# A fused attention and SwiGLU kernel: its pieces put in order by a list scheduler, in even blocks of 512 tokens

## The chip, the cores and the metric

One core of a Trainium2 chip. The core has a matrix engine (TensorE, PE in the rows; PEld is its weight load), a vector engine (DVE), an activation engine (ACT), GpSimd (POOL) and SP, which here only issues DMAs. Each engine works through its own queue in order and waits at semaphores for the others. The metric is the device time of one execution in microseconds (us); lower is better.

## The reference

Attention with normalised queries and keys (batch 8, 12 heads, 448 tokens, head size 64), then a SwiGLU feed-forward network over its 3584 tokens (768 to 1536 to 768), all in fp32:

```python
q_n, k_n = (rmsnorm(q, g_q), rmsnorm(k, g_k))
scores = scale * np.matmul(q_n, k_n.transpose(0, 1, 3, 2))
scores = scores - np.max(scores, axis=-1, keepdims=True)
attn = np.exp(scores)
attn = attn / (np.sum(attn, axis=-1, keepdims=True) + 1e-09)
x = np.matmul(attn, v)            # then to (tokens, heads * head size)
g = x @ w_gate
silu = g * (1.0 / (1.0 + np.exp(-g)))
val = x @ w_val
return (silu * val @ w_out).astype(np.float32)
```

The weights arrive as 64-bit floats, and the kernel turns them into fp32 itself.

## The kernel before

The launch has two versions in it: `fast`, which runs on this input, and `general` behind a test of the gains at the end. Everything below is about `fast`. Lines are those of the kernel before.

**Attention** goes by pairs of heads, 6 pairs to a batch, 48 in all (index m). For a pair, `normalise` squares q and k on ACT (L511), sums on DVE (L515, L516), takes the power -1/2 on POOL (tile rr, L518) and scales q and k on POOL (tile t, L522). `transpose_qk` turns t round on PE (L539); the copies QT (DVE, L544) and KT (ACT, L548) leave PSUM. `scores` makes, for each quarter j of the keys, two products (L555, tile st), an exponential on ACT (L563, tile e), and on POOL the running sum of e over j (L566, L568, tile sums). `weighted` multiplies the four e with v (L575, tile at). `divide` multiplies sums with a matrix of ones (L588), so that each row holds the denominators, inverts them (DVE RECIPROCAL, L590, tile inv) and writes the quotient to xT (L591). The pool of at has two buffers, for the product with v, the denominators and the transposes; st has two, e five.

**The network** goes by blocks of tokens. xT holds two batches (896 tokens), cut into a block of 384 and one of 512. A block has an up phase, 24 groups of 6 products (L622, tile mm, with `wg` for gates and `wv` for values, tanh on ACT at L633, two DVE steps at L634 and L638 into gt), and a down phase (L648, `wo`; 3 or 4 times 2 groups of 12 products), whose rows ACT copies out (L658) and stores. An fp32 product is two PE rows in the trace.

**The weights** come in 36 parts of 768 KB. `load_weights` puts a part into one of four places within gt; `round_weights` converts it: two ACT steps (L480, L481) and four DVE steps (L482, L483, L491, L494) for each part.

**The order** is the order of the Python calls, the same on all engines. `slot(i)` issues half a pair; `attend(n)` issues n slots, each with one step of the weights (two in slots 8 to 13); `mix` puts slots between the groups of a block. Seven pairs of attention run before the first up phase; six pairs lie in each even up phase (384 tokens), six in each odd down phase; even down phases and odd up phases have none:

```python
    attend(PER + 2)
    for n in range(B):
        if n % 2 == 0:
            mix(ups(n), PER)
...
            mix(downs(n), 0)
        else:
            mix(ups(n), 0)
            mix(downs(n), PER if n < B - 1 else 0)
```

Of the kernel before, what the change touches and what calls it, by code (L numbers as in the profile page):

```python
# [359 lines left out]

@with_exitstack
def fast(
# [23 lines left out]

# [12 lines left out]
    BLOCKS = ((0, 384), (384, 512))  # L399
    TB = 512  # L400

    const = ctx.enter_context(tc.tile_pool(name="const", bufs=1))
    io = ctx.enter_context(tc.tile_pool(name="io", bufs=2))
    prep = ctx.enter_context(tc.tile_pool(name="prep", bufs=2))
    attn = ctx.enter_context(tc.tile_pool(name="attn", bufs=1))
    ffn = ctx.enter_context(tc.tile_pool(name="ffn", bufs=2))
    ps_st = ctx.enter_context(tc.tile_pool(name="ps_st", bufs=2, space=bass.MemoryType.PSUM))
    ps_at = ctx.enter_context(tc.tile_pool(name="ps_at", bufs=2, space=bass.MemoryType.PSUM))
    ps_mm = ctx.enter_context(tc.tile_pool(name="ps_mm", bufs=2, space=bass.MemoryType.PSUM))
    ctx.enter_context(tc.manual_schedule())  # L410

# [3 lines left out]
    xT = const.tile([P, NW, 2 * S], F32, name="xT")  # L415
# [7 lines left out]

    qk, vt, qkn, QT, KT, E, sums, av = ({} for _ in range(8))

# [4 lines left out]
    def load_qk(m):  # L432
        if m < NM:
            for x, src in enumerate((q, k)):
                qk[m, x] = io.tile([R, 2, NJ, D], F32, name="qk", bufs=3)
                nc.sync.dma_start(qk[m, x].rearrange("p h j d -> p h (j d)"), pair_rows(src, m))

    def load_v(m):
        if m < NM:
            vt[m] = io.tile([R, 2, NJ, D], F32, name="v")  # L440
            nc.sync.dma_start(vt[m].rearrange("p h j d -> p h (j d)"), pair_rows(v, m))
# [8 lines left out]
    def weight_parts():  # L450
        gate, val = (w.rearrange("(c p) f -> p c f", p=P) for w in (moe_w_gate, moe_w_val))
        for f in range(NF // 2):
            for half in range(2):
                for w, dst in ((gate, wg), (val, wv)):
                    cs = ts(half, NW // 2)
                    yield w[:, cs, ts(f, 2 * P)], dst[:, f, cs, :], (NW // 2, 2 * P)
        rows = moe_w_out.rearrange("(f p) c -> p f c", p=P)
        for f in range(NF):
            yield rows[:, f : f + 1, :], wo[:, f : f + 1, :], (1, DM)

    def load_weights():
        if not parts:
            return
        n = parts[0][0]
        slot = n % 4 if n < 20 else 2 + n % 2
        if any(slot == other[0] for other in staged):
            return
        _, (src, dst, (a, b)) = parts.pop(0)
        raw = gt[:, ts(slot, NF // 4), :].rearrange("p f t -> p (f t)").bitcast(I64)
        raw = raw.rearrange("p (a b) -> p a b", a=a)  # L470
        nc.sync.dma_start(raw, src)
        words = raw.bitcast(U32).rearrange("p a (b two) -> p a b two", two=2)
        staged.append((slot, words[:, :, :, 0], words[:, :, :, 1], dst))

    def round_weights():
        if not staged:
            return
        _, lo, hi, w = staged.pop(0)
        bits = w.bitcast(U32)
        nc.scalar.activation(w, hi.bitcast(F32), AF.Abs)  # L480
        nc.scalar.activation(lo, lo, AF.Copy, scale=2.0**-29)  # L481
        nc.vector.tensor_scalar_max(w, w, LEAST)  # L482
        nc.vector.tensor_scalar(  # L483
            out=bits,
            in0=bits,
            scalar1=3,
            scalar2=0x3FFFFFFF,
            op0=ALU.logical_shift_left,
            op1=ALU.bitwise_and,
        )  # L490
        nc.vector.scalar_tensor_tensor(  # L491
            bits, hi, 0xC0000000, bits, op0=ALU.bitwise_and, op1=ALU.bitwise_or
        )
        nc.vector.tensor_tensor(out=bits, in0=bits, in1=lo, op=ALU.add)  # L494

    def weights_step():
        round_weights()
        load_weights()
# [3 lines left out]
    def normalise(m):  # L502


        if m >= NM:
            return
        src = [qk.pop((m, x)) for x in range(2)]
        t = prep.tile([R, NJ, 2, 2, D], F32, name="t")
        sq = t.rearrange("p j x h d -> p (j x h d)").rearrange("p (g d) -> p g d", d=D)
        for x in range(2):  # L510
            nc.scalar.activation(  # L511
                sq[:, ts(x, 2 * NJ)], src[x].rearrange("p h j d -> p (h j) d"), AF.Square
            )
        ss = prep.tile([R, 2 * 2 * NJ], F32, name="ss")
        nc.vector.tensor_reduce(out=ss, in_=sq, axis=AX.X, op=ALU.add)  # L515
        nc.vector.tensor_scalar_add(ss, ss, D * 1e-6)  # L516
        rr = prep.tile([R, 2, 2, NJ, 1], F32, name="rr")
        nc.gpsimd.tensor_tensor(  # L518
            out=rr.rearrange("p x h j one -> p (x h j one)"), in0=ss, in1=minus_half, op=ALU.pow
        )  # L520
        for x in range(2):
            nc.gpsimd.tensor_tensor(  # L522
# [7 lines left out]
    def transpose_qk(m):  # L530
        if m >= NM:
            return
# [280 lines left out]
```

## Time and profile before

| | us |
|---|---|
| median of three runs | 1924.35 |
| lowest, highest run | 1920.6, 1932.96 |
| the profiled execution, its own time | 1931.18 |
| span of its trace (first to last instruction) | 1929.4 |

The profile is of one execution. Its span leaves 1.8 us of that execution's time outside. In the rows below, a time line gives start, duration, engine, line, operation, output and inputs with their shapes, a count, and in brackets the idle time in front with what ended it. The end of a PE row is modelled, so lengths on PE are best read from one start to the next. PEclk is the clock granted to TensorE as a share of 2.4 GHz.

### The profile page before, as it was taken

The numbers are of one execution on the slowest core, as the hardware profiler recorded it, in microseconds if no ns is written. First come the engines' busy times: TensorE is split into PE (matmuls) and PEld (weight loads), VectorE is DVE, ScalarE is ACT, GpSimd is POOL, SyncE is SP. The second block draws the span as 40 slices with busy tenths as digits, with TensorE's granted clock in tenths as the row PEclk, the third lists the DMA queues.
The fourth block names the chain that finished last, engine by engine and source line by source line (L and its number), as shares of the span: only waits on it lengthen the run. The fifth ranks groups of instructions, "written<-read, shape, count | busy, mean of one in ns | idle before, by whom it ended". The sixth has DMA issues, their size and how long they took to land.

```text
span 1929.4 us, 14302 instructions
## 1 busy us (share of the span) xinstructions
PE 1773.2 (92%) x5760; PEld 867.0 (45%) x5760; DVE 530.3 (27%) x580; ACT 382.1 (20%) x561; POOL 550.6 (29%) x296
## 2 busy tenths in 40 slices
PE   4557669999989999999999899999999899999998
PEld 1223335544444455554444455554444445554455
DVE  4997563101122233201112233301112232201100
ACT  4353332100023222100022222200012222100000
POOL 5753224300035444400024544410015444200000
PEclk9778779999999999999999999999999899999999
DMA  4353330100011111000011110010001110000000
GB/s 155 116 160 106 112 113 29 32 13 0 0 37 46 47 29 29 24 21 0 0 33 41 41 29 29 29 30 0 0 17 47 37 38 20 2 21 4 0 9 26
DMA packets 55247, 73.37 MB, mean 38 GB/s; under 512 B 4996, under 2 KB 44420, under 8 KB 55172
## 3 DMA queue, kind: packets, MB, share of 16 engines
q1 hardware_dynamic: 45888, 61.35, 10.2%
q10 hardware_dynamic: 9284, 11.02, 2.0%
q8 instruction: 47, 0.77, 0.2%
q14 instruction: 28, 0.23, 0.0%
HBM read 61.34 MB, written 11.01 MB: 38 GB/s over the span
## 4 chain that ended last, share of the span: by engine, by line
PE 85%; POOL 5%; DVE 5%; issue 3%; ACT 1%; DMA 1%; POOLq 0%; SPq 0%; DVEq 0%; ACTq 0%
PE mm L622 44%; PE mm L648 20%; PE st L555 9%; PE at L575 8%; POOL rr L518 3%; POOL t L522 2%; PE at L539 2%; PE at L588 2%; DVE inv L590 1%; DMA gt<-in_moe_w_out_dram 1%; ACT e L563 1%; DVE wg L494 0%; DVE wg L483 0%; DVE wo L494 0%; DVE wg L491 0%
## 5 line engine op out<-in xcount | busy, mean ns | idle before, releaser
L622 PE MATMUL mm<-xT,wg 128*128 128x512 f32 (+1 forms) x1152 | 455.4, 544 | 7.8 <-DVE xT L591 7.8
L622 PE MATMUL mm<-xT,wv 128*128 128x512 f32 (+1 forms) x1152 | 450.4, 541 | 0.0
L648 PE MATMUL mm<-wo,gt 128*128 128x384 f32 x1344 | 444.0, 489 | 0.0
L566 POOL TENSOR_TENSOR sums<-e 112x896 f32<-112x896 f32 x48 | 102.2, 2129 | 1094.8 <-ACT e L563 850.5
L648 PEld LDWEIGHTS mm<-wo,gt 128*128 128x128 f32 x1344 | 252.3, 190 | 195.2 <-issue 27.3
L622 PEld LDWEIGHTS mm<-xT,wg 128*128 128x128 f32 x1152 | 214.8, 190 | 244.6 <-issue 168.3
L622 PEld LDWEIGHTS mm<-xT,wv 128*128 128x128 f32 x1152 | 219.9, 191 | 215.3 <-issue 139.9
L563 ACT ACTIVATE e<-st 112x896 f32<-112x896 f32 x192 | 170.9, 916 | 215.1 <-PE st L555 167.2
L568 POOL TENSOR_TENSOR sums<-sums,e 112x896 f32<-112x896 f32 x96 | 206.7, 2153 | 16.8 <-ACT e L563 12.9
L634 DVE SCALAR_TENSOR_TENSOR gt<-tanh,mm 128x384 f32<-128x384 f32 (+1 forms) x96 | 59.6, 620 | 530.8 <-ACT tanh L633 530.8
L555 PE MATMUL st<-QT,KT 64*112 64x448 f32 x768 | 195.5, 633 | 0.1
L590 DVE RECIPROCAL inv<-at 128x448 f32<-128x448 f32 x48 | 141.9, 2956 | 162.8 <-PE at L588 162.8
L575 PE MATMUL at<-e,v 112*64 112x448 f32 x768 | 167.3, 581 | 16.5 <-ACT KT L548 16.5
L633 ACT ACTIVATE tanh<-mm 128x384 f32<-128x384 f32 (+1 forms) x96 | 52.2, 543 | 648.3 <-PE mm L622 648.3
L539 PE MATMUL at<-ident,t 112*128 112x112 f32 x384 | 61.5, 306 | 126.6 <-POOL t L522 80.1
L518 POOL TENSOR_TENSOR rr<-ss,minus_half 112x16 f32<-112x16 f32 x48 | 143.8, 2996 | 12.0 <-DVE ss L516 12.0
L638 DVE SCALAR_TENSOR_TENSOR gt<-gt,mm 128x384 f32<-128x384 f32 (+1 forms) x96 | 59.6, 621 | 301.4 <-PE mm L622 301.4
L539 PEld LDWEIGHTS at<-ident,t 112*128 112x128 f32 x384 | 47.6, 163 | 153.3 <-POOL t L522 96.3
L575 PEld LDWEIGHTS at<-e,v 112*64 112x64 f32 x768 | 54.1, 146 | 132.5 <-issue 106.2
L515 DVE TENSOR_REDUCE ss<-t 112x16 f32<-112x1024 f32 x48 | 58.5, 1220 | 200.6 <-ACT t L511 200.6
L555 PEld LDWEIGHTS st<-QT,KT 64*112 64x112 f32 x768 | 68.8, 195 | 83.8 <-issue 66.7
L658 ACT COPY rows<-mm 128x384 f32<-128x384 f32 x56 | 26.8, 479 | 402.2 <-PE mm L648 402.2
(37 smaller groups left out, 521.6 us busy)
## 6 DMA issues: line engine op xcount, KB each, us to landing
qk<-in_q_dram SPq DMA_DIRECT2D x48, 224.0 KB, 3.0
qk<-in_k_dram SPq DMA_DIRECT2D x48, 224.0 KB, 2.6
v<-in_v_dram SPq DMA_DIRECT2D x48, 224.0 KB, 2.8
gt<-in_moe_w_gate_dram SPq DMA_DIRECT2D x12, 768.0 KB, 4.6
gt<-in_moe_w_val_dram SPq DMA_DIRECT2D x12, 768.0 KB, 4.9
gt<-in_moe_w_out_dram SPq DMA_DIRECT2D x12, 768.0 KB, 4.5
out_dram<-rows ACTq DMA_DIRECT2D x16, 168.0 KB, 2.2
out_dram<-rows ACTq DMA_DIRECT2D x16, 144.0 KB, 2.1
```

The costliest lines, as they stand in the source:

```text
L518: nc.gpsimd.tensor_tensor(out=rr.rearrange("p x h j one -> p (x h j one)"), in0=ss, in1=minus_half, op=ALU.pow)
L539: nc.tensor.transpose(ps[:, ts(j, R)], t[:, j, x].rearrange("p h d -> p (h d)"), ident[0:R, 0:R])
L555: nc.tensor.matmul(st[0:R, h, 0:S], KT[m][rows, j, :], QT[m][rows].rearrange("p j r -> p (j r)"), start=True, stop=True,)
L563: nc.scalar.activation(E[m, j], st[0:R, :, 0:S], AF.Exp)
L566: nc.gpsimd.tensor_tensor(out=sums[m], in0=E[m, 0], in1=E[m, 1], op=ALU.add)
L568: nc.gpsimd.tensor_tensor(out=sums[m], in0=sums[m], in1=E[m, j], op=ALU.add)
L575: nc.tensor.matmul(av[m][ds(D * h, D), 0:S], vt[m][:, h, j, :], e[:, h], start=(j == 0), stop=(j == NJ - 1),)
L590: nc.vector.reciprocal(inv, den[:, 0:S])
L622: nc.tensor.matmul(ps[:, 0:size], w[:, f // 2, c, ts(f % 2, P)], xT[:, c, ds(at, size)], start=(c == 0), stop=(c == NW - 1),)
L634: nc.vector.scalar_tensor_tensor(g, t[:, 0:size], 1.0, ps[:, 0:size], op0=ALU.add, op1=ALU.mult)
L638: nc.vector.scalar_tensor_tensor(g, g, 0.5, ps[:, 0:size], op0=ALU.mult, op1=ALU.mult)
L648: nc.tensor.matmul(ps[:, 0:HALF], gt[:, f, ts(i, P)], wo[:, f, ts(half, HALF)], start=(f == 0), stop=(f == NF - 1),)
```

## The change

`fast` no longer calls its steps in the order of the work. It describes each step as a piece (`Order.add`): the engine, an assumed duration, a wished time, the pieces it must follow, the buffers it takes and uses. `Order.run` then picks, again and again, the piece that can start first by its own account of the five engines, among the pieces of an engine by wished time, and emits it. The order on each engine is thus fixed when the kernel is built; on the chip each engine still runs its queue in order.

Besides the order, the change alters the work itself:

- Blocks: seven of 512 tokens, and xT is a ring of 1024 tokens. The quotient of a pair (L754 of the kernel after) may only be written when the up phase of the block that had its place is over (`up_done`). Batches 0 and 1 (12 pairs, "early") all precede the first up phase; the pairs of later batches are wished into the down phases, those of the last batch across block 5.
- Sums over keys: for the early pairs, each e is multiplied with the matrix of ones on PE as it is multiplied with v (16 PE rows for a pair where there were 4), and POOL adds nothing. Later pairs keep the sums on POOL.
- Weights: ten staging places, four in gt and six in wo, where there were four in gt.
- Transposes take a buffer of st instead of two of at; a pair takes two of at, one for the product with v and one for the denominators. e has four buffers instead of five, the q and k loads four instead of three.
- Half of the early QT copies go to ACT. tanh writes into gt in place. The four small loads of the gains go through POOL's queue instead of ACT's, and one exponential is issued at the start.

```diff
+class Order:
...
+    def start(self, piece):
+        at = self.free.get(piece["engine"], 0.0)
+        if piece["port"]:
+            at = max(at, self.port)
+        for before in piece["after"]:
+            if before["end"] is None:
+                return None
+            at = max(at, before["end"] + 0.1)
+        for name, _ in piece["takes"]:
+            old = self.pools[name][self.turn[name] % len(self.pools[name])]
+            for user in self.users.get(old, ()):
+                if user["end"] is None:
+                    return None
+                at = max(at, user["end"] + 0.1)
+        return at
+    def run(self, lookahead=400):
+        left = {}
+        for piece in sorted(self.pieces, key=lambda p: (p["when"], p["n"])):
+            left.setdefault(piece["engine"], []).append(piece)
+        while any(left.values()):
+            best = None
+            for engine, pieces in left.items():
+                choice = None
+                for piece in pieces[:lookahead]:
+                    at = self.start(piece)
+                    if at is not None and (choice is None or at < choice[0] - 0.02):
+                        choice = (at, piece)
+                if choice and (best is None or choice[0] < best[0]):
+                    best = choice
+            at, piece = best
+            left[piece["engine"]].remove(piece)
+            for key in piece["takes"]:
+                ring = self.pools[key[0]]
+                ring[self.turn[key[0]] % len(ring)] = key
+                self.turn[key[0]] += 1
+            end = at + piece["us"]
+            self.free[piece["engine"]] = end
+            if piece["port"]:
+                self.port = end
+            if piece["kb"]:
+                self.dma = max(self.dma, end) + piece["kb"] / 300.0
+                end = self.dma + 1.8
+            piece["at"], piece["end"] = at, end
+            piece["emit"]()
...
+    NB = B * S // TB
+    RING = 2 * TB
+    EARLY = 2 * NPAIR
...
+    BUFS = dict(qk=4, v=2, t=2, QT=2, KT=2, e=4, sums=1, inv=1, rows=2, st=2, at=2, mm=2, ss=2, rr=2)
...
+    xT = const.tile([P, NW, RING], F32, name="xT")
...
+    LEAD, PAIR = 14.0, 10.5
+    FIRST = LEAD + EARLY * PAIR + 10.0
+    UP, DOWN, BOTH = 122.0, 63.0, 113.0
+    def block_start(n):
+        return FIRST + n * (UP + BOTH)
+    def pair_time(m):
+        b, c = divmod(m, NPAIR)
+        if m < EARLY:
+            return LEAD + m * PAIR, PAIR
+        n = b - 2
+        if b == B - 1:
+            return block_start(n) + c * 28.0, 28.0
+        return block_start(n) + UP + (c - 1) * BOTH / NPAIR, BOTH / NPAIR
...
+        ex, adds = [], []
+        for j in range(NJ):
+            when = base + (j // 2) * span * 0.4 + (j % 2) * 0.1
...
+            if j and not early:
+                adds.append(
+                    add(
...
+        def weighted(j):
+            if j == 0:
+                take("at", (m, "av"), [P, TB])
+            if j == 0 and early:
+                take("at", (m, "den"), [P, TB])
+            e = tiles["e", (m, j)]
+            x = tiles["v", m]
+            product("av", lambda h: x[:, h, j, :], e, j == 0, j == NJ - 1)
+            if early:
+                product("den", lambda h: ones[0:R, :], e, j == 0, j == NJ - 1)
...
+        if not early:
+            def total():
+                take("at", (m, "den"), [P, TB])
+                product("den", lambda h: ones[0:R, :], tiles["sums", m], True, True)
...
+        blocks = range(
+            max(0, (b * S - RING) // TB), max(0, -(-((b + 1) * S - RING) // TB))
+        )
+        done_x[m] = add(
+            "DVE", 0.66, base + span + 1.0, divide, after=[inv] + [up_done[n] for n in blocks],
+            uses=[av, ("inv", m)],
...
+                    where = n % 10
+                    stage = ("gt", where) if where < 4 else ("wo", where - 4)
...
+            stage = ("wo", (5, 4, 3)[f % 3]) if f < 8 else ("gt", 2 + f % 2)
...
+                        "PE", 5.05, start + (2 * f + which) * step,
+                        lambda f=f, which=which: gate_value(f, which),
+                        after=[done_x[m] for m in tokens]
+                        + (weights["gv"[which], f // 2] if n == 0 else []) + [last],
+                        takes=[("mm", (n, f, which))],
...
+                    "PE", 3.93, start + UP + (2 * g + part) * span,
+                    lambda i=i, half=half, part=part: out_rows(i, half, part),
+                    after=[*hidden[part * NF // 2 : (part + 1) * NF // 2], last]
...
+    nc.scalar.activation(warm, minus_half[:, 0:1], AF.Exp)
     for t, x in ((gq2, g_q), (gk2, g_k)):
         col = x.rearrange("(d one) -> d one", one=1)
-        nc.scalar.dma_start(t[0:64, :], col)
-        nc.scalar.dma_start(t[64:128, :], col)
-    load_v(0)
-    nc.gpsimd.memset(minus_half, -0.5)
+        nc.gpsimd.dma_start(t[0:64, :], col)
+        nc.gpsimd.dma_start(t[64:128, :], col)
...
+    for b in range(2):
+        for c in range(NPAIR):
+            attention(b * NPAIR + c)
+    for n in range(NB):
+        block(n)
+        if n + 2 < B:
+            for c in range(NPAIR):
+                attention((n + 2) * NPAIR + c)
+    order.run()
```

Where it moves instructions, at three places. First DVE in the early stretch, (L482 to L494 and L828 to L852 are the four steps of a part of the weights, L515/L516 and L579/L580 the sums of squares, inv and xT the end of a pair). Before:

```order
L515 TENSOR_REDUCE ss_524<-t_521 112x16
L516 TENSOR_SCALAR ss_524<-ss_524 112x16
L482 TENSOR_SCALAR wg_93<-wg_93 128x768
L483 TENSOR_SCALAR wg_93<-wg_93 128x768
L491 SCALAR_TENSOR_TENSOR wg_93<-gt_97,wg_93 128x768
L494 ISA wg_93<-gt_97,wg_93 128x1536
L482 TENSOR_SCALAR wv_94<-wv_94 128x768
L483 TENSOR_SCALAR wv_94<-wv_94 128x768
L491 SCALAR_TENSOR_TENSOR wv_94<-gt_97,wv_94 128x768
L494 ISA wv_94<-gt_97,wv_94 128x1536
L590 RECIPROCAL inv_564<-at_561 128x448
L591 TENSOR_TENSOR xT_96<-at_510,inv_564 128x448
```

After:

```order
L579 TENSOR_REDUCE ss_713<-t_695 112x16
L580 TENSOR_SCALAR ss_713<-ss_713 112x16
L852 ISA wv_79<-wo_80,wv_79 128x1536
L833 TENSOR_SCALAR wg_78<-wg_78 128x768
L828 TENSOR_SCALAR wv_79<-wv_79 128x768
L845 SCALAR_TENSOR_TENSOR wg_78<-wo_80,wg_78 128x768
L833 TENSOR_SCALAR wv_79<-wv_79 128x768
L852 ISA wg_78<-wo_80,wg_78 128x1536
L845 SCALAR_TENSOR_TENSOR wv_79<-wo_80,wv_79 128x768
L744 RECIPROCAL inv_757<-at_698 128x448
L852 ISA wv_79<-wo_80,wv_79 128x1536
L754 TENSOR_TENSOR xT_81<-at_697,inv_757 128x448
```

Before, two whole parts stand between the sums of squares of one pair and the end of another; after, the steps of two parts are woven into each other and a pair's steps are placed among them one by one.

Second, PE in a down phase with attention: block 1 before, block 0 after (mm with wo are the down groups). Before:

```order
L648 MATMUL mm_2020<-wo_95,gt_97 128x384 x6
L555 MATMUL st_2088<-QT_1934,KT_1935 112x448 x2
L555 MATMUL st_2094<-QT_1934,KT_1935 112x448 x2
L588 MATMUL at_2100<-sums_1958,ones_99 64x448 x2
L648 MATMUL mm_2106<-wo_95,gt_97 128x384 x12
L539 MATMUL at_2125<-ident_98,t_2064 128x112 x4
L539 MATMUL at_2131<-ident_98,t_2064 128x112 x4
L555 MATMUL st_2137<-QT_2027,KT_2028 112x448 x2
L555 MATMUL st_2142<-QT_2027,KT_2028 112x448 x2
```

After:

```order
L658 MATMUL st_1638<-QT_1447,KT_1445 112x448 x2
L705 MATMUL at_1643<-sums_1396,ones_84 64x448 x2
L658 MATMUL st_1648<-QT_1447,KT_1445 112x448 x2
L932 MATMUL mm_1655<-wo_80,gt_82 128x384 x6
L705 MATMUL at_1668<-e_1607,v_1367 64x448 x2
L620 MATMUL st_1671<-ident_83,t_1214 128x112 x8
L705 MATMUL at_1668<-e_1622,v_1367 64x448 x2
L932 MATMUL mm_1655<-wo_80,gt_82 128x384 x6
L705 MATMUL at_1668<-e_1646,v_1367 64x448 x2
```

Before, a pair's work comes in two lumps, with its transposes right in front of its scores; after, transposes, scores and products with v are single pieces among half groups of six down products, and the transposes in the middle belong to a pair whose scores come later.

Third, PE where a down phase ends and the next up phase begins (L622 and L872). Before:

```order
L648 MATMUL mm<-wo,gt 128x384 x6
L555 MATMUL st<-QT,KT 112x448 x4
L588 MATMUL at<-sums,ones 64x448 x2
L622 MATMUL mm<-xT,wg 128x384 x6
L622 MATMUL mm<-xT,wv 128x384 x6
```

After:

```order
L620 MATMUL st<-ident,t 128x112 x8
L705 MATMUL at<-sums,ones 64x448 x2
L658 MATMUL st<-QT,KT 112x448 x8
L620 MATMUL st<-ident,t 128x112 x8
L872 MATMUL mm<-xT,wg 128x512 x6
L705 MATMUL at<-e,v 64x448 x2
```

Before, the up phase follows directly on the last product with ones; after, four quarters of scores and a pair's transposes stand between the two.

## Rows read from the trace of the kernel before

**Rows 1.** The page: the span, and PE's busy time over it.

```profile
span 1929.4 us, 14302 instructions
...
PE 1773.2 (92%) x5760; PEld 867.0 (45%) x5760; DVE 530.3 (27%) x580; ACT 382.1 (20%) x561; POOL 550.6 (29%) x296
```

**Rows 2.** Windows: span, busy us by engine (instructions), PEclk, DMA share, GB/s.

```profile
0.00:178.00 178.00, 93.46 (x352) 39.45 (x352) 138.90 (x134) 78.90 (x107) 102.94 (x56) 0.80 0.44 140
...
525.00:662.00 137.00, 126.44 (x467) 59.96 (x465) 34.65 (x31) 34.38 (x50) 59.04 (x32) 0.94 0.14 40
662.00:804.00 142.00, 141.98 (x544) 72.63 (x545) 43.73 (x53) 36.66 (x54) 63.60 (x36) 1.00 0.10 30
50.00:60.00 10.00, 6.06 (x20) 2.75 (x22) 9.76 (x6) 1.45 (x2) 9.83 (x5) 0.51 0.33 103
```

**Rows 3.** Chain of waits, in order of time: start us, length us, what.

```profile
401.56 123.60 PE mm L622 x288
...
658.34 2.97 DVE inv L590
...
1862.19 61.93 PE mm L648 x192
```

**Rows 4.** Timeline of DVE in the first 180 us.

```profile
7.23 1.21 DVE L515 TENSOR_REDUCE ss<-t 112x16 f32<-112x1024 f32 x1
...
30.36 0.55 DVE L482 TENSOR_SCALAR wg<-wg 128x768 f32<-128x768 f32 x1
30.94 0.56 DVE L483 TENSOR_SCALAR wg<-wg 128x768 uint32<-128x768 uint32 x1
...
33.51 0.57 DVE L482 TENSOR_SCALAR wv<-wv 128x768 f32<-128x768 f32 x1
...
39.78 0.67 DVE L544 TENSOR_SCALAR QT<-at,gg 128x448 f32<-128x448 f32 x1
43.44 1.22 DVE L515 TENSOR_REDUCE ss<-t 112x16 f32<-112x1024 f32 x1 [2.99 <-ACT t L511]
...
44.78 0.55 DVE L482 TENSOR_SCALAR wg<-wg 128x768 f32<-128x768 f32 x1
...
47.06 2.63 DVE L494 CUSTOM_DVE_ANT_0 wg<-gt,wg 128x1536 uint16<-128x1536 uint16 x1
49.61 2.94 DVE L590 RECIPROCAL inv<-at 128x448 f32<-128x448 f32 x1
...
53.13 0.86 DVE L482 TENSOR_SCALAR wv<-wv 128x768 f32<-128x768 f32 x1
...
90.94 0.86 DVE L482 TENSOR_SCALAR wv<-wv 128x768 f32<-128x768 f32 x1
91.84 1.28 DVE L483 TENSOR_SCALAR wv<-wv 128x768 uint32<-128x768 uint32 x1
```

**Rows 5.** Timeline of POOL in the first 180 us.

```profile
46.31 2.56 POOL L566 TENSOR_TENSOR sums<-e 112x896 f32<-112x896 f32 x1 [4.51 <-PE at L588]
...
90.35 2.35 POOL L522 TENSOR_TENSOR t<-qk,rr 112x512 f32<-112x512 f32 x2
```

**Rows 6.** Timeline of PE in the up phase of block 2.

```profile
669.19 3.23 PE L575 MATMUL at<-e,v 112*64 112x448 f32 x16
672.35 4.14 PE L622 MATMUL mm<-xT,wg 128*128 128x384 f32 x12
...
680.28 1.76 PE L555 MATMUL st<-QT,KT 64*112 64x448 f32 x8
681.98 0.97 PE L588 MATMUL at<-sums,ones 112*64 112x448 f32 x4
682.88 4.14 PE L622 MATMUL mm<-xT,wg 128*128 128x384 f32 x12
...
690.72 0.93 PE L539 MATMUL at<-ident,t 112*128 112x112 f32 x8
691.58 1.76 PE L555 MATMUL st<-QT,KT 64*112 64x448 f32 x8
```

More of the change, by code (lines that the diff above doesn't have):

```diff
@@ L358, in general, with __init__, add @@
             fn()
+class Order:
+    def __init__(self, pools):
+        self.pools = {name: [None] * n for name, n in pools.items()}
+        self.turn = dict.fromkeys(pools, 0)
+        self.users = {}
+        self.pieces = []
+        self.free = {}
+        self.port = 0.0
+        self.dma = 0.0
+    def add(self, engine, us, when, emit, after=(), takes=(), uses=(), port=False, kb=0):
+        piece = dict(
+            engine=engine, us=us, when=when, emit=emit, takes=takes, port=port, kb=kb,
+            after=[a for a in after if a is not None], end=None, n=len(self.pieces),
+        )
+        for tile_of in (*takes, *uses):
+            self.users.setdefault(tile_of, []).append(piece)
+        self.pieces.append(piece)
+        return piece
+    def start(self, piece):
[42 more added lines that the diff above has]
+            piece["emit"]()
@@ new lines, in fast, with weight_part @@
+    weights = {}
+    staged = {}
+    def weight_part(n, src, dst, shape, what, stage):
+        a, b = shape
+        before = staged.get(stage)
+        when = 8.0 + 5.0 * n
+        region, s = stage
+        if region == "gt":
+            raw = gt[:, ts(s, NF // 4), :].rearrange("p f t -> p (f t)")
+        else:
+            raw = wo[:, ts(s, 2), :].rearrange("p f c -> p (f c)")
+        raw = raw.bitcast(I64).rearrange("p (a b) -> p a b", a=a)
+        words = raw.bitcast(U32).rearrange("p a (b two) -> p a b two", two=2)
+        lo, hi = words[:, :, :, 0], words[:, :, :, 1]
+        bits = dst.bitcast(U32)
+        add = order.add
+        loaded = add(
+            "SP", 0.45, when - 14.0, lambda: nc.sync.dma_start(raw, src), after=[before], kb=768
+        )
+        clear = [staged.get(("wo", what[1] // 2))] if what[0] == "o" else []
+        one = add(
+            "ACT", 0.91, when, lambda: nc.scalar.activation(dst, hi.bitcast(F32), AF.Abs),
+            after=[loaded, *clear],
+        )
+        two = add(
+            "ACT", 0.91, when, lambda: nc.scalar.activation(lo, lo, AF.Copy, scale=2.0**-29),
+            after=[loaded],
+        )
+        three = add(
+            "DVE", 0.56, when, lambda: nc.vector.tensor_scalar_max(dst, dst, LEAST),
+            after=[one], port=True,
+        )
+        four = add(
+            "DVE", 0.57, when,
+            lambda: nc.vector.tensor_scalar(
+                out=bits,
+                in0=bits,
+                scalar1=3,
+                scalar2=0x3FFFFFFF,
+                op0=ALU.logical_shift_left,
+                op1=ALU.bitwise_and,
+            ),
+            after=[three], port=True,
+        )
+        five = add(
+            "DVE", 0.97, when,
+            lambda: nc.vector.scalar_tensor_tensor(
+                bits, hi, 0xC0000000, bits, op0=ALU.bitwise_and, op1=ALU.bitwise_or
+            ),
+            after=[four], port=True,
+        )
+        six = add(
+            "DVE", 0.97, when,
+            lambda: nc.vector.tensor_tensor(out=bits, in0=bits, in1=lo, op=ALU.add),
+            after=[five, two], port=True,
+        )
+        staged[stage] = six
+        weights.setdefault(what, []).append(six)
```

534 lines of the change are left out of this document (282 added, 252 removed).

## The prediction

> **What bounds the kernel now.** I read the page first: PE is busy for 1773.2 of 1929.4 us [rows 1]. That looks like a matrix-bound kernel with 8% to win, but busy time also counts slow and half-waiting products. So the next view is the chain of waits, which holds stretches where PE does nothing but one kind of product: 288 rows of an up phase of 512 tokens in 123.60 us, 192 rows of a down phase of 512 tokens in 61.93 us [rows 3]. From these I get the rate of PE when nothing is late: 0.429 us for a row of 512 columns, 0.323 us for one of 384. The timeline of PE gives the attention, from start to start [rows 6]: 16 rows with v 3.16 us (669.19 to 672.35), 8 rows of scores 1.70, the 4 rows with ones 0.90, the 8 transposes 0.86. A pair has two lots of scores: 3.16 + 2 x 1.70 + 0.90 + 0.86 = 8.32 us.
>
> With these the whole of before can be added up. Up phases: 4 x 123.6 + 4 x 288 x 0.323 = 866. Down phases: 7 x 61.93 = 434 (3584 tokens). Pairs: 48 x 8.32 = 399. A run of products of the network that is broken off for attention loses a little: 24 rows took 7.93 and 7.84 us [rows 6] where 24 x 0.323 is 7.74, about 0.15; 85 such runs by the order give 13. With 5.3 us from the last product (1862.19 + 61.93) to the end of the span that makes 1717. So 212 of 1929 us are waiting or slow clock. Where? Block 1's up phase starts at 401.56 [rows 3]; by then PE has done 13 pairs (108), an up phase of 384 (93) and a down phase of 384 (46), some 250 with its breaks: about 150 us are lost there. The window of a down phase with attention has 137 us [rows 2] for eight groups (62), six pairs (50) and breaks (1): 24 lost; there are three such phases, 72 us. The up phase with six pairs, 662 to 804, has PE busy for 141.98 of 142: nothing lost. 150 + 72 is the 212, within its rounding.
>
> In the first 178 us DVE is busy for 138.90 and PE for 93.46, at a mean clock of 0.80 [rows 2]; in 50 to 60 us DVE has 9.76 of 10 and PE runs at 0.51. DVE bounds that stretch.
>
> **The early stretch after.** All twelve pairs of batches 0 and 1 now come before the first product of the network. By the order, DVE issues up to the twelfth quotient: 32 of the 36 parts of the weights, 14 sums of squares, 12 ends of pairs, 8 copies QT. Start to start in rows 4: a part 3.15 (30.36 to 33.51, undisturbed), a sum 1.34 (43.44 to 44.78), an end 3.52 (49.61 to 53.13), a copy 0.67. Sum: 100.8 + 18.8 + 42.2 + 5.4 = 167 us, on top of a first instruction at about 7 us: 174.
>
> To this comes POOL. While POOL added up e for 2.56 us from 46.31 [rows 5], the last step of a part took 2.63 us [rows 4]; while it scaled t, from 90.35, two steps took 0.86 and 1.28 instead of 0.55 and 0.56, so 1.0 us more. The sums of the early pairs leave POOL, the scaling stays: 14 x 1.0 = 14. The bounds are 0 (POOL under a DVE step that doesn't mind) and its full length, 14 x 2.35 = 33; I take 14, since it is the row of the very operation. The Trainium skill ("SBUF — State Buffer", section "SBUF: two separate sides") says that DVE in certain forms and GpSimd lock a shared pair of ports for a whole instruction and the other blocks fully. By that rule the 33 would hold and the total would be 19 us higher; the rows of the scaling show less, since part of it fell under the quotient.
>
> Then DVE's own waits: nearly none in 50 to 60 us, 32 of the 171 us after its start in the first 178 [rows 2]. The new order puts steps of ready weights between those of pairs, so I take 12, with 0 and 40 as bounds. The early stretch: 174 + 14 + 12 = **200 us** (174 to 247). PE hides under it: per pair 8.32 + 12 further rows with ones at 3.16/16 = 10.7, twelve times 128, and at the mean clock of before (0.80) 160. The ten staging places let the loads run ahead; they can't beat DVE's 3.15 us for a part. The loads of the gains on POOL's queue and the added exponential lie ahead of the first sum of squares, where by the order POOL only fills constants; I count 0, between a gain of 1 and a loss of 7, which is all that lies before that sum [rows 4].
>
> **The rest after.** PE's work from the first product on: seven up phases 865, seven down phases 434, 36 pairs 300. Blocks of 512 instead of 384 gain 1 us, no more. The finer cutting costs: by the order 176 runs of network products are broken off, x 0.15 = 26; scores stand in 105 runs and products with v or ones in 180, where 72 and 72 are in the 8.32; each further run costs 0.11 (four rows with ones 0.90 instead of 0.79), 141 x 0.11 = 16. Off goes what the order shows done early, five quarters of scores and two transposes: 6. Sum **1635** (1593 if cutting is free).
>
> Waits between: three places can stall PE. The quotient of a later pair waits for `up_done`; behind it in DVE's queue stand the next inverse and the next copies, and for these waits PE. But the quotient is issued after the last gate of that up phase, so it is due at once, and half a down group (12 x 0.323 = 3.9 us) covers it. At the end of a down phase the up phase needs inverse and quotient, 3.52 us: before, nothing covered it (2.97 of inverse stands bare in the chain [rows 3]); now four quarters of scores and the transposes, 2 x 1.70 + 0.86 = 4.3, stand in between. Transposes no longer stand right before their own scores. So I expect most of the 24 us of such a phase to go. Bounds: 0 for a pair (662 to 804) and 24/6 = 4 (525 to 662), for 36 pairs 0 to 144. I take **20**, near the lower row, because each stall that made the upper one has something else to do in front of it.
>
> Sum: 200 + 1635 + 20 + 5.3 = 1860 span, + 1.8 outside = **1862 us**, against the 1931.18 of the execution that the rows come from; that lies 0.35% over the median of 1924.35, and I don't scale. In other words: PE gets some 55 us more work (1774 against 1717), and waits fall from 212 to 86.
>
> **Rivals.**
> - The lists don't fit the chip (slower). The order was made from assumed durations, and every queue runs in order: where an exponential, a POOL sum or a store in ACT's queue is late, PE stands before a ready group. For it: the down phases get a pair every 20 us, and 525 to 662, with one per 23, lost 24. Against it: the up phase with 24 us for a pair lost nothing. At 4 us for a pair the sum is 1862 + 124 = 1986; it is slower by 1% from 2.8 us for a pair.
> - PE stays at the lower clock (1.2 GHz) through the early stretch (no change to slower). Twelve pairs at 10.7 and the 6 us done early, all at half speed, are 268 us, with 7 in front 275 instead of 200: 1937. For it: 0.51 in 50 to 60 us. Against it: PE's share of that stretch rises from 93 of 178 to about 134 of 200, and 0.80 was the mean even before. The Trainium skill ("TensorE: Matmul & The Clock Gate", section "HAM oscillation") says that bursts with waits between them fall back to the lower clock again and again; the trace agrees so far as 0.51 goes.
> - DVE takes more: the scaling blocks for its full length (33 in place of 14, +19) and DVE waits for 40 instead of 12: 1909. Still some 1% faster at most, so this one is near no change. It is also the way in which the change wouldn't do what it says: more staging and sums on PE leave the early stretch as long as DVE makes it.
> - Better than forecast: cutting is free (-42), waits 0 (-20): 1800.
>
> **How the numbers follow.** A measurement here tells about 1% from no change: 1905 to 1944 around the median. Forecast (1835 to 1890) 0.58; better 0.18; DVE between forecast and its rival 0.10, of which 0.06 below 1905; PE cold 0.06, two thirds of it short of 1944; the lists 0.08, a quarter of it short of 1944. Faster 0.58 + 0.18 + 0.06 = 0.82; same 0.04 + 0.04 + 0.02 = 0.10; slower 0.02 + 0.06 = 0.08. The range leaves out the far end of the better case (below 1805) and the far ends of the slower ones: 1805 to 1930.
>
> **What would show it.** In the trace after: the first network product near 200 us with DVE over 90% busy before it, and the last step of a part seldom over 2 us; the chain in steady state all PE; up phases with attention at clock 1.00; down phases with five pairs near 108 us; the span from the first network product to the end near 1660. It is wrong if PE's waits for POOL or ACT in down phases sum to over 60 us, if the first product comes after 235 us, or if the runs cut into four rows take much more than 0.9 us.

## The result, and the profile after

The changed kernel takes **1863.07 us** (median of four runs, 1862.21 to 1865.27) where the kernel before took 1925.23 in the same session: ratio 0.9675, 95% interval 0.9642 to 0.9708. The forecast was 1862. The profiled execution took 1865.27 us. The rows of after follow; first the page, against [rows 1].

```profile
span 1863.5 us, 13867 instructions
...
PE 1806.0 (97%) x5616; PEld 780.7 (42%) x5616; DVE 497.3 (27%) x568; ACT 387.6 (21%) x556; POOL 507.2 (27%) x264
```

PE is busy 33 us longer than before in a span that is 66 us shorter: it does more work and waits less. The chain of waits, against [rows 3] (start, length, what, and how many PE rows stand there without a break):

```profile
200.36 5.35 PE mm L872 x12
...
1796.16 61.93 PE mm L932 x192
```

The first network product comes at 200.36, and from there to the end it is 1663.1 us. The same chain, for 200.3 to 1863.5 alone, by line:

```profile
by line: PE mm L872 53.0%; PE mm L932 27.1%; PE at L705 9.5%; PE st L658 7.2%; PE st L620 1.9%; ACT e L668 0.6%; DVE QT L641 0.2%; ACT KT L633 0.2%; issue 0.1%; ACT rows L942 0.1%; ACTq L668 0.0%
```

The five PE entries are 98.7%, 1642 us; 21 us go to everything else, the tail of 5.4 among it. PE's timeline against [rows 6], first in a down phase with attention and then between this phase and the next up phase:

```profile
339.93 0.97 PE L705 MATMUL at<-e,v 112*64 112x448 f32 x4
340.83 4.14 PE L932 MATMUL mm<-wo,gt 128*128 128x384 f32 x12
344.90 0.97 PE L705 MATMUL at<-e,v 112*64 112x448 f32 x4
...
438.85 0.97 PE L705 MATMUL at<-sums,ones 112*64 112x448 f32 x4
440.26 1.76 PE L658 MATMUL st<-QT,KT 64*112 64x448 f32 x8 [0.44 <-DVE QT L641]
442.35 1.82 PE L658 MATMUL st<-QT,KT 64*112 64x448 f32 x8 [0.33 <-ACT e L668]
444.44 0.98 PE L620 MATMUL st<-ident,t 112*128 112x112 f32 x8 [0.27 <-ACT e L668]
445.26 5.33 PE L872 MATMUL mm<-xT,wg 128*128 128x512 f32 x12
```

From the product with ones (438.85) to the up phase (445.26) nothing waits for the inverse: scores and transposes cover it. One wait for a copy QT and two for exponentials cost 1.0 us together.

The early stretch, windows of 50 us against [rows 2] (span, then busy us of PE, PEld, DVE, ACT, POOL with the number of instructions, then PEclk, DMA share, GB/s):

```profile
0.00:50.00 50.00, 25.11 (x112) 9.54 (x112) 30.17 (x41) 31.80 (x43) 17.74 (x19) 1.00 0.97 285
50.00:100.00 50.00, 41.55 (x188) 15.89 (x190) 41.80 (x53) 40.30 (x54) 40.69 (x16) 0.83 0.68 204
100.00:150.00 50.00, 43.55 (x208) 14.47 (x204) 42.02 (x51) 26.66 (x37) 38.67 (x15) 0.97 0.35 107
150.00:200.00 50.00, 44.03 (x206) 14.95 (x204) 42.73 (x52) 31.61 (x42) 15.92 (x7) 0.93 0.47 152
```

DVE is busy for 156.7 of these 200 us, 78%; before, it had 9.76 of 10 at 50 us [rows 2]. No engine is full, and PE's clock falls to 0.83 in the second window. DVE's timeline at its start and at two woven parts, against [rows 4]:

```profile
13.66 0.16 DVE L991 SCALAR_TENSOR_TENSOR gg<-gq,gk 128x1 f32<-128x1 f32 x1 [9.53 <-DMA gk<-in_g_k_dram]
13.74 1.21 DVE L579 TENSOR_REDUCE ss<-t 112x16 f32<-112x1024 f32 x1
...
42.74 0.55 DVE L828 TENSOR_SCALAR wv<-wv 128x768 f32<-128x768 f32 x1
43.21 0.55 DVE L828 TENSOR_SCALAR wg<-wg 128x768 f32<-128x768 f32 x1
43.68 0.55 DVE L833 TENSOR_SCALAR wv<-wv 128x768 uint32<-128x768 uint32 x1
44.15 0.55 DVE L833 TENSOR_SCALAR wg<-wg 128x768 uint32<-128x768 uint32 x1
44.62 0.95 DVE L845 SCALAR_TENSOR_TENSOR wv<-wo,wv 128x768 uint32<-128x768 uint32 x1
45.49 0.95 DVE L845 SCALAR_TENSOR_TENSOR wg<-wo,wg 128x768 uint32<-128x768 uint32 x1
```

The first sum of squares starts at 13.74, not at 7.23: gg, ahead of it in DVE's queue, waits for the gains. Steps of two parts follow each other every 0.47 us where steps of one part took 0.58 [rows 4]. POOL's timeline against [rows 5]:

```profile
57.99 10.30 POOL L588 TENSOR_TENSOR rr<-ss,minus_half 112x16 f32<-112x16 f32 x1 [3.76 <-DVE ss L580]
...
72.56 2.90 POOL L588 TENSOR_TENSOR rr<-ss,minus_half 112x16 f32<-112x16 f32 x1 [2.15 <-DVE ss L580]
75.53 4.25 POOL L600 TENSOR_TENSOR t<-qk,rr 112x512 f32<-112x512 f32 x2
80.60 5.35 POOL L588 TENSOR_TENSOR rr<-ss,minus_half 112x16 f32<-112x16 f32 x1 [0.82 <-DVE ss L580]
```

The power rr, 2.90 us where nothing disturbs it, takes up to 10.30 here. Four of the fourteen before 200 us take 7.55 to 10.30, two more 4.01 and 5.35; the mean is 4.9.

### The profile page after: what moved, and what is told of

Read it like the earlier page. It is cut to its first block, busy times and chain, and to the rows that moved or that the text cites. A ratio compares the mean times of both kernels' runs of the same rounds, so it can differ in the third digit from the quotient of the medians.

```text
span 1863.5 us, 13867 instructions
## 1 busy us (share of the span) xinstructions
PE 1806.0 (97%) x5616; PEld 780.7 (42%) x5616; DVE 497.3 (27%) x568; ACT 387.6 (21%) x556; POOL 507.2 (27%) x264
## 3 DMA queue, kind: packets, MB, share of 16 engines
q1 hardware_dynamic: 45888, 61.35, 11.1%
## 4 chain that ended last, share of the span: by engine, by line
PE 92%; issue 3%; POOL 2%; ACT 1%; DVE 1%; ACTq 0%; POOLq 0%
PE mm L872 47%; PE mm L932 24%; PE at L705 11%; PE st L658 8%; PE st L620 2%; POOL rr L588 1%; POOL t L600 1%; ACT e L668 1%; DVE inv L744 0%; DVE QT L641 0%; ACT KT L633 0%; DVE wo L852 0%; DVE wo L845 0%; ACT wo L820 0%; ACT wo L824 0%
## 5 line engine op out<-in xcount | busy, mean ns | idle before, releaser
L872 PE MATMUL mm<-xT,wv 128*128 128x512 f32 x1008 | 450.7, 596 | 0.6 <-ACT rows L942 0.6
L872 PE MATMUL mm<-xT,wg 128*128 128x512 f32 x1008 | 450.3, 596 | 0.0
L872 PEld LDWEIGHTS mm<-xT,wv 128*128 128x128 f32 x1008 | 188.0, 190 | 249.8 <-issue 248.6
L674 POOL TENSOR_TENSOR sums<-e 112x896 f32<-112x896 f32 x36 | 75.2, 2089 | 790.2 <-ACT e L668 790.2
L872 PEld LDWEIGHTS mm<-xT,wg 128*128 128x128 f32 x1008 | 187.8, 190 | 244.1 <-issue 222.4
L882 ACT ACTIVATE gt<-mm 128x512 f32<-128x512 f32 x84 | 50.2, 597 | 689.4 <-PE mm L872 689.4
L677 POOL TENSOR_TENSOR sums<-sums,e 112x896 f32<-112x896 f32 x72 | 149.5, 2076 | 128.2 <-ACT e L668 126.1
L885 DVE SCALAR_TENSOR_TENSOR gt<-gt,mm 128x512 f32<-128x512 f32 x84 | 57.7, 687 | 435.9 <-ACT gt L882 435.9
L890 DVE SCALAR_TENSOR_TENSOR gt<-gt,mm 128x512 f32<-128x512 f32 x84 | 57.7, 687 | 338.9 <-PE mm L872 338.9
L600 POOL TENSOR_TENSOR t<-qk,rr 112x512 f32<-112x512 f32 x96 | 110.5, 1170 | 3.2
L641 DVE TENSOR_SCALAR QT<-st,gg 128x448 f32<-128x448 f32 x42 | 28.5, 678 | 254.9 <-ACT KT L633 254.5
L620 PE MATMUL st<-ident,t 112*128 112x112 f32 x384 | 50.0, 273 | 34.8 <-POOL t L600 31.9
```

The costliest lines, as they stand in the source:

```text
L600: nc.gpsimd.tensor_tensor(out=tiles["t", m][:, :, x].rearrange("p j h d -> p h j d"), in0=tiles["qk", (m, x)], in1=tiles["rr", m][:, x].to ...
L620: nc.tensor.transpose(ps[:, x, ts(j, R)], tiles["t", m][:, j, x].rearrange("p h d -> p (h d)"), ident[0:R, 0:R],)
L674: nc.gpsimd.tensor_tensor(out=to, in0=tiles["e", (m, 0)], in1=e, op=ALU.add)
L677: nc.gpsimd.tensor_tensor(out=to, in0=to, in1=e, op=ALU.add)
L872: nc.tensor.matmul(ps, w[:, f // 2, c, ts(f % 2, P)], xT[:, c, ts(n % 2, TB)], start=(c == 0), stop=(c == NW - 1),)
L885: nc.vector.scalar_tensor_tensor(gt[:, f], gt[:, f], 1.0, tiles["mm", (n, f, 0)], op0=ALU.add, op1=ALU.mult)
```

## The experiments

Where nothing else is said a kernel is the changed one with the edit shown; `...` in an edit marks lines left out. Each median comes with its ratio to the kernel before on the same chip.

**The changed kernel again.**

> The changed kernel itself, unaltered, on the chip of the next three: 1858 to 1868 us, ratio to the kernel before 0.962 to 0.971. It says whether the chip of these runs moves the ratio; all theories expect the same.

1864.69 us, ratio 0.967 (0.9649 to 0.9691), first product at 198.2: the yardstick for the rest.

**The gains on ACT's queue.**

```diff
-        nc.gpsimd.dma_start(t[0:64, :], col)
+        nc.scalar.dma_start(t[0:64, :], col)
```

(and the same for the other half)

> The kernel after with one edit: the four small loads of the gains go through ACT's queue again instead of POOL's. In the trace of the kernel after, DVE's first sum of squares starts at 13.74 us behind the product of the gains, which waited 9.53 us for these loads; before it started at 7.23 us. If the early stretch is set by the amount of work on DVE (the forecast), all of the 6.5 us come back: about 1857 us. If it is set later, by POOL's powers, which are held up (7.5 to 10.3 us instead of 2.9 for six of fourteen), DVE only waits longer there: 1860 to 1863 us.

1859.91 us, ratio 0.9623 (0.9607 to 0.9639). The first sum starts at 11.70 instead of 13.74, the first product at 196.80 instead of 200.36. By time this is the edge of the second theory, but only 2.0 of the 6.5 us came back at the start, which neither theory had. The move to POOL's queue costs these 2 us at the start and 3 to 5 in all; it was counted at 0.

**Four staging places instead of ten.**

```diff
-                    where = n % 10
-                    stage = ("gt", where) if where < 4 else ("wo", where - 4)
+                    stage = ("gt", n % 4)
...
-            stage = ("wo", (5, 4, 3)[f % 3]) if f < 8 else ("gt", 2 + f % 2)
+            stage = ("gt", 2 + f % 2)
```

> The kernel after with four staging places in gt instead of ten in gt and wo; nothing else. If DVE's amount sets the early stretch, a place is free again after landing (4 to 5 us), two ACT steps (1.8) and four DVE steps (3 to 4), so four places still bring a part each 2.7 us where DVE needs about 2.7 to 3.2: 1863 to 1870 us. If the ten places are what keeps ready steps in front of DVE, DVE waits for loads: about 20 us more, 1883 us.

1861.14 us, ratio 0.9633 (0.9617 to 0.9649), first product at 193.81: 2 us below the first theory's range. The ten places bring nothing. With the gains moved as well:

> Gains on ACT's queue and four staging places, both at once. Theory A (each takes something off the early stretch on its own: e1 3.6 us, e3 6.5 us to the first product): first product near 190, 1855 to 1859 us. Theory B (each change only shuffles the list's order, so nothing adds up): 1858 to 1866 us, first product 193 to 201.

1857.25 us, ratio 0.9634 (0.9612 to 0.9656), first product at 191.65: within theory A's range. To the first product the two save 8.7 us together and 3.6 and 6.5 alone; the ratios of the three runs can't be told apart.

**The steps of a part in one piece**, so that the list can't weave two parts:

```diff
-        three = add(
-            "DVE", 0.56, when, lambda: nc.vector.tensor_scalar_max(dst, dst, LEAST),
-            after=[one], port=True,
-        )
...
+        def words_to_float():
+            nc.vector.tensor_scalar_max(dst, dst, LEAST)
...
+        six = add("DVE", 3.07, when, words_to_float, after=[one, two], port=True)
```

> The kernel after with the four DVE steps of a part of the weights as one piece, so that they stand together as before the change; nothing else. In the trace of the kernel after woven steps follow each other with 0.47 us for a step of 0.55 (start to start), where steps of one part take 0.58 to 0.59, so a part costs about 2.7 us instead of 3.15. Theory A (DVE's amount sets the stretch): 32 x 0.47 = 15 us more: 1878 us. Theory B (dense woven steps hold up POOL's powers, and the chain runs through these): the small gaps between dependent steps let POOL in, powers fall back to 2.9 to 3.6 us, and the time stays or falls: 1855 to 1863 us.

1887.28 us, ratio 0.9766 (0.9749 to 0.9782), first product at 223.62. The window from 50 to 100 us, and POOL's power before 240 us:

```profile
50.00:100.00 50.00, 31.11 (x142) 11.73 (x138) 48.76 (x55) 34.89 (x47) 23.73 (x12) 0.83 0.66 193
```

```profile
L588 POOL TENSOR_TENSOR rr<-ss,minus_half 112x16 f32<-112x16 f32 x16 | 50.3, 3146 | 125.5 <-DVE ss L580 125.5
```

POOL is free again (3146 ns), yet the kernel is 23 us slower: DVE is full (48.76 of 50). That is theory A's direction, 9 us above its figure. The rest is that the list now puts all 36 parts and 16 sums of squares before the twelfth quotient, where the changed kernel has 32 and 14: four parts and two sums are 15 us at the forecast's prices, the missing weave another 15, and DVE's busy time before the first product rises by 31 (157.0 to 187.9). So the run shows that this stretch pays for what is put on DVE. It shows neither the price of the weave alone nor that POOL's long powers cost nothing.

**Early sums on POOL again.** The products with ones leave PE for the early pairs. To avoid a deadlock over the two buffers of at, a pair's first product with v also follows the pair before's product with ones.

```diff
+        onpe = False
...
-            if j and not early:
+            if j and not onpe:
                 adds.append(
...
-            if early:
+            if onpe:
                 product("den", lambda h: ones[0:R, :], e, j == 0, j == NJ - 1)
...
+                lambda j=j: weighted(j), after=[ex[j], load_v, last, prev_total.get(m - 1)],
...
+            prev_total[m] = last
```

> The kernel after with the early pairs' sums over keys added up on POOL again, as before the change, and one product with ones per pair; nothing else. 36 additions of 2.1 us come to POOL in the early stretch, 144 PE rows less on TensorE (28 us of work that the forecast holds for hidden). Forecast's theory (DVE's amount sets the stretch, POOL's additions stop DVE): up to 36 x 1.7 = 61 us on DVE if each addition holds up a step, half of it likely: about 1890 us, the first product of the network near 230 us. Rival (POOL is the one that is held up, and the chain runs through POOL): POOL gets 77 us more work in the same queue as the powers, each held up in turn: 1900 us or more, with powers of 7 us and over becoming the rule. Third: the products with ones are worth nothing, 1863 within 4 us.

1938.94 us, ratio 1.0036 (1.0024 to 1.0049): the whole gain is gone. First product at 275.83. Its window from 50 to 100 us, and the two longest sums of PE's waits before 276 (us in total, times, longest):

```profile
50.00:100.00 50.00, 2.62 (x8) 0.41 (x8) 46.28 (x59) 25.81 (x33) 39.69 (x8) 0.56 0.54 175
```

```profile
PE at L707 <- DVE inv L747: 43.8, 8, 31.5
PE at L707 <- POOL sums L679: 35.0, 4, 30.9
```

PE does 2.62 us of work in 50; eight instructions of POOL fill 39.69. By time this is the rival (1900 us or more). Its sign did not come: the powers before 240 us are 4.5 us on the mean, not over 7 as a rule. How much of the loss is due to the order that the edit puts on the pairs was not separated.

**Both of these edits.**

> The early sums over keys on POOL again (as in e2) and the four DVE steps of a part in one piece (as in e5). Theory A (with the sums on POOL, the early stretch is long because POOL's operations are held up under woven DVE steps, and PE waits for POOL): unweaving sets POOL free, its sums fall from 5 us to near 3, and the kernel comes out clearly below e2, 1895 to 1915 us, first network product near 240. Theory B (it is long because POOL's and DVE's work together is too much whatever the weave): 1940 to 1965 us, first product 275 to 300. The second is the sum of the two losses, 76 + 24 on top of 1863.

1935.50 us, ratio 1.0038 (1.0022 to 1.0055), first product at 270.87. Neither theory: POOL is freed (a power 3.2 us, a further sum 2.2), but PE then waits 64.6 us for inverses behind a DVE that is full (48 of 50). With sums on POOL one engine or the other is late.

**The list looks at two pieces of an engine**, those wished first, instead of 400:

```diff
-    def run(self, lookahead=400):
+    def run(self, lookahead=2):
```

> The list looks at the first two pieces of an engine by wished time instead of 400; pieces, costs and wished times are the same. Theory A (the gain lies in the sums on PE and in wished times that spread the pieces; the choice by readiness adds little): 1863 to 1885 us, most of the difference before the first network product. Theory B (the choice by readiness is what removes the waits): DVE and ACT wait at the head of their queues for parts and pairs in turn, first product 230 to 260 us and 20 to 60 us of new waits in the down phases, 1910 to 1980 us.

1855.36 us, ratio 0.9621 (0.96 to 0.9642). Neither theory: the time is below both ranges. As in A the difference lies before the first product, but the short list gains there; as in B there are new waits in the down phases. The up phase stands in the chain as one unbroken piece from 167.57; after it, one row of PE's waits:

```profile
167.57 98.05 PE mm L872 x228
```

```profile
PE st L658 <- DVE QT L641: 31.2, 17, 2.6
```

The same wait is 2.2 us in the changed kernel from its first product on. So the choice by readiness takes 29 us of these waits out of the down phases, and the first network product comes 31 to 33 us later with it. To take the one without the other:

```diff
-                for piece in pieces[:lookahead]:
+                near = 2 if pieces and pieces[0]["when"] < 150.0 else lookahead
+                for piece in pieces[:near]:
```

> The list looks at two pieces of an engine while the first of them is wished before 150 us, and at 400 afterwards. Theory A (early, the choice by readiness fills DVE with steps of parts that the first network product does not need, 31 parts before the twelfth quotient against 27, and so holds up the pairs, which cost the 31 us between 198 and 167; later it saves the waits of PE for QT, 31 us in e8_lookahead_2): first network product near 168, waits of PE after it under 10 us, 1833 to 1840 us. Theory B (the short list early only moves the conversion of weights behind the first product, where it then meets the down phases' attention, as the 27 us between e8's 1855 and 168 + 1665 may also show): 1848 to 1860 us, with waits for DVE after 168 of 15 us or more.

**1840.77 us**, ratio 0.9539 (0.9516 to 0.9563), 1.3% below the changed kernel: theory A, a microsecond over its bound. This is the better order in what follows. Its chain, its windows, and PE's waits after 170:

```profile
168.02 36.44 PE mm L873 x84
```

```profile
50.00:100.00 50.00, 46.31 (x238) 16.82 (x236) 47.57 (x53) 36.70 (x50) 22.60 (x14) 1.00 0.56 190
...
7.00:167.00 160.00, 135.14 (x668) 48.82 (x670) 137.69 (x161) 106.87 (x144) 70.24 (x36) 1.00 0.57 186
```

```profile
PE st L659 <- DVE QT L642: 2.2, 5, 0.4
```

From the first product to the end of the span it is 1684.2 us with two pieces throughout and 1671.0 here: of the 29 us of waits only 13 come out as time. For the same rows PE is busy for 12 us more (1658.9 against 1646.9), since the choice by readiness cuts the work finer, and waits of other kinds grow by 4 us. The changed kernel's 1663.1 has 6 us of work done ahead.

In this order the parts of the weights are not woven. DVE's timeline, and PE's longest sum of waits before the first product, here (L621) and in the changed kernel (L620):

```profile
53.79 0.55 DVE L829 TENSOR_SCALAR wg<-wg 128x768 f32<-128x768 f32 x1
54.37 0.56 DVE L834 TENSOR_SCALAR wg<-wg 128x768 uint32<-128x768 uint32 x1
54.97 0.96 DVE L846 SCALAR_TENSOR_TENSOR wg<-wo,wg 128x768 uint32<-128x768 uint32 x1
56.06 0.96 DVE L853 CUSTOM_DVE_ANT_0 wg<-wo,wg 128x1536 uint16<-128x1536 uint16 x1
```

```profile
PE st L621 <- POOL t L601: 20.6, 1, 20.6
```

```profile
PE st L620 <- POOL t L600: 31.9, 8, 20.8
```

The one wait of some 20 us is the start of the program. The seven others of the changed kernel, 11.1 us, are gone here, and no power takes over 4.01 us, though DVE is busier from 50 to 100 us (47.57 against 41.80).

Up to the first product PE is busy for some 136 us here and 154 in the changed kernel, and idle for 32 and 46. Of the 18 us of busy time 6 are work done ahead; the other 12 are products at the lower clock (0.83 against 1.00 in the second window) or half waiting. Of the 14 us of idle time 11 are the waits for POOL's t.

> The same with the gains on ACT's queue. Theory A (the gains are on the way to the first sum of squares and all pairs follow it): 2 to 4 us below the run without, first product near 165. Theory B (at a pace of 10.5 us for a pair wished by the list, a start 2 us earlier is swallowed by the next wait): within 1 us of it.

1839.70 us, ratio 0.9531 (0.9509 to 0.9554), first product at 168.46: theory B. The earlier start (11.91 against 13.56 for the first sum of squares) is swallowed. By what isn't shown: the profiled execution, the slowest of the four, has PE at a clock of 0.91 from 100 to 120 us, where the run without has 1.00.

**That order with the early sums on POOL.**

> The order of e10_near_two_early with the early sums over keys on POOL (the edit of e2). Theory A (the products with ones are worth their 28 us of PE work under any order: POOL would have 3.4 for a power, 2.4 for the two scalings and 6.3 for three sums, 12.1 us for a pair where the early pace is 11.9, and each sum stands in front of an inverse): first network product 190 to 230 us, 1862 to 1900 us. Theory B (e2 lost its gain by the list's order, not by POOL's load; in an order that follows the wished times the sums hide on POOL, and PE has less to do): first product 160 to 175, 1832 to 1847 us.

1892.00 us, ratio 0.9804 (0.9766 to 0.9842), first product at 218.40: theory A. DVE's timeline at one part of the weights, and POOL's at the same time:

```profile
62.04 1.78 DVE L832 TENSOR_SCALAR wg<-wg 128x768 f32<-128x768 f32 x1 [1.03 <-ACT wg L824]
63.85 2.41 DVE L837 TENSOR_SCALAR wg<-wg 128x768 uint32<-128x768 uint32 x1
66.29 2.74 DVE L849 SCALAR_TENSOR_TENSOR wg<-wo,wg 128x768 uint32<-128x768 uint32 x1
68.95 1.21 DVE L582 TENSOR_REDUCE ss<-t 112x16 f32<-112x1024 f32 x1
```

```profile
61.30 2.10 POOL L677 TENSOR_TENSOR sums<-e 112x896 f32<-112x896 f32 x1 [1.79 <-ACT e L671]
63.74 4.47 POOL L680 TENSOR_TENSOR sums<-sums,e 112x896 f32<-112x896 f32 x2 [0.34 <-ACT e L671]
```

Three steps that take 0.55, 0.55 and 0.95 us alone take 6.93 together; POOL adds beside them for 5.8 of its 6.57 us. The Trainium skill ("SBUF — State Buffer", section "SBUF: two separate sides") calls the pair of ports that certain DVE forms and GpSimd share an exclusive lock for a whole instruction. The trace agrees in kind: 4.9 us come on top of DVE's own work while POOL adds for 5.8.

**Fewer parts early.**

```diff
-    LEAD, PAIR = 14.0, 10.5
+    LEAD, PAIR = 14.0, 9.8
-        when = 8.0 + 5.0 * n
+        when = 8.0 + 5.6 * n
```

(in the kernel with 1840.77 us; the two edits stand at different places)

> e10_near_two_early with a pair wished each 9.8 us instead of 10.5 and a part of the weights each 5.6 instead of 5.0; by the order 23 parts instead of 27 then stand before the twelfth quotient. Theory A (DVE's amount still holds up the early stretch, at 47.6 of 50 us busy): first product 158 to 164, 1831 to 1837 us. Theory B (PE is the bound now: 10.7 us of products for a pair, 46.3 of 50 us busy): first product 165 to 168 and within 3 us of 1841.

1839.26 us, ratio 0.9532 (0.9495 to 0.9569): within 1.5 us of it, first product at 167.54: theory B. From 50 to 100 us:

```profile
50.00:100.00 50.00, 47.48 (x238) 16.38 (x234) 41.39 (x47) 34.47 (x48) 24.28 (x14) 1.00 0.55 173
```

DVE has 8 us to spare and nothing is gained: PE, at full clock, is the bound of the early stretch now.

## Why the prediction was right, and where it was not

**The rest after the first product: right by its own steps.** Work 1635 and waits and tail 25 were forecast, 1642 and 21 are in the chain. The price of cutting holds: between the down groups four rows take 0.90 us from start to start (339.93 to 340.83), as forecast, and twelve rows of a down group 4.07 (340.83 to 344.90), 0.20 over the unbroken 3.87 where 0.15 was forecast. The waits of a down phase went for the reason given: something else stands in front of each. The two-piece list shows these waits without it, 31 us. No wait of PE after the first product is longer than 0.6 us, so the rival of ill-fitting lists fell here. Other signs came as named: the last step of a part is never over 1.79 us before the twelfth quotient, and the first down phase with pairs takes 109.3 us (335.96 to 445.26) where 108 was said.

**The early stretch: 200 forecast, 200.36 measured, by errors that cancel.** No term of "174 + 14 + 12" came true, and that the sum did is luck. Measured: DVE's first step for a pair at 13.7, not 7 (+6.7); DVE busy for 156 us after it, not 167 + 14 (-25); DVE waiting for the remaining 30 or so, not 12 (+18).
- *The start.* The loss of 7 us had been the far bound, with 0 taken. That POOL only fills constants did not help: the product of the gains (gg) stands ahead of the first sum in DVE's queue, as before the change, and waits for the loads. The queue is only 2 of the 6.5 us; with the gains on ACT's queue again gg still starts at 11.63, and at 7.15 in the kernel before. The likely rest is that SP now issues the first part of the weights (768 KB) at 1.67 us, before the change at 13.16; on ACT's queue the gains' loads land after 6.4 to 8.4 us, before the change after 3.1 to 4.2. No run tried it.
- *The parts.* The 3.15 us came from a row in which each step follows its own predecessor. Woven, a part takes two spacings of 0.47 and two of 0.87, 2.7 us: 14 us less for 32 parts.
- *The contention.* Not 14 us but 3: the four steps of a part are 3.09 us long on the mean of the 32, 3.00 undisturbed. The scaling hardly disturbs a woven run of DVE steps; the run holds POOL up instead, which has no term in the sum. These 11 us and the 14 of the parts are the -25.
- *The waits.* "DVE over 90% busy" was the sign of the forecast, and the trace has 78%. 17 of DVE's 30 us of waiting are for products of PE, and PE waited for POOL. In the chain of the changed kernel the long powers stand bare:

```profile
107.50 7.56 POOL rr L588
...
119.93 8.97 POOL rr L588
```

The list counts a power as 3.0 us and lets it run beside DVE's steps, so it could not see this. It started whatever could start first and so wove ready parts (32 before the twelfth quotient, 27 in the better order) in front of steps of pairs that PE waited for. The order is what costs the 32 us, as the two-piece list shows. How they divide between the held powers, the five further parts and the lower clock was not separated; no run frees the powers and changes nothing else.

One sum on the kernel before doesn't close: 150 + 72 is 222, not the 212 that it was to explain. Nothing in the forecast hangs on the ten.

**The rivals.** PE at the lower clock came in part: 12 us at most, not the 75 of its sum. "DVE takes more" did not come by its first cause, the contention; its waits of DVE came by two thirds. The better case was open after all, but by another way than free cutting: through the early stretch, down to 1840.

**What the change's parts are worth.** Sums as products with ones: 51 us in the better order, 71 to 76 in its own (both with the order on the pairs that the edit adds). Choice by readiness: some 13 us gained late; early the first product comes 32 us later, 6 of them work done ahead. Ten places and gains on POOL's queue: nothing, or a few us lost. Blocks of 512 and the ring were not tried alone.

## What to carry to other kernels

A list scheduler that starts whatever is ready first fills an engine's queue with work that nobody needs yet. Here free choice lost where much such filler was ready (the weights, early) and gained where none was left (the down phases); follow the wished order in the first case. When work can leave a slower engine for the matrix unit, count what the slower engine's traffic does to its neighbour, not only its own time; and where two engines hold each other up, the list's account needs that too. Fewer waits are not the same as less time: 29 us of waits were worth 13. A total that comes out right proves none of its terms: read the sign that each term was to show.

## What was not expected of the hardware

- DVE steps that don't depend on the one before start 0.47 us apart where dependent ones start 0.58 apart (128x768).
- A power on 112x16 values on POOL, 2.90 us alone, took 10.30 beside a run of woven DVE steps, over many of them and not just one. All six powers over 4 us in the changed kernel's early stretch ended 2.75 to 2.76 us after the last step of such a run had ended (65.53 and 68.29 for the longest): as if they had begun only then. Beside parts that are not woven none took over 4.01 (the better order).
- With the gains' loads on POOL's queue gg started at 13.66 us, on ACT's at 11.63: 2 us for four loads of 256 bytes.
